# Block-product experts: the third product's copy taken ahead of the ReLU, the first two experts' weight work dealt anew, two maxima sent together

## The chip, the cores and the metric

The kernel runs on one core of one Trainium2 chip. The metric is the time of one execution on the device in microseconds (us), lower is better. Profiles are of single executions, taken by the hardware profiler. PE is the engine that multiplies matrices (TensorE), PEld its weight load, DVE the vector engine, ACT the scalar engine, POOL is GpSimd, SP the engine whose queue issues every DMA of this kernel. "n" below counts products of weights, "e" experts.

## What is computed

Attention, then a small dense layer, then eight experts that all see every token; the gate P is normalised by rows and columns eight times.

```python
def _moe2_ref(x, w_gate, w1, w2) -> np.ndarray:      # x (1152, 512), w1 (8, 512, 1024), w2 (8, 1024, 512)
    logits = x @ w_gate
    logits = logits - logits.max()
    P = np.exp(logits)
    for _ in range(8):
        P /= P.sum(1, keepdims=True) + 1e-09
        P /= P.sum(0, keepdims=True) + 1e-09
        P *= N / E
    out = np.zeros((N, D), dtype=np.float32)
    for e in range(E):
        h = np.maximum(x @ w1[e], 0.0)
        ye = h @ w2[e]
        out += P[:, e:e + 1] * ye
    return out.astype(np.float32)
```

The change lies in the experts alone.

## The kernel before

The kernel is one long program whose order is written out by hand: on each engine instructions run in the order in which the program issues them, and an instruction that waits holds all behind it. Every float32 matrix is split into a high and a low float16 part, and each product is the sum of three matmuls (high by high, high by low, low by high), scaled by powers of two that follow from the largest magnitude of each weight matrix.

**First matmul of an expert.** A column block n of w1 (four per expert, `up(n)`, n = 0 to 31) is a 2 by 2 block product with seven block products in place of eight (`prod`, L1229, 12 matmuls each), in the order x (A11 B11), z (A12 B21), y (S1 T1), x (S2 T2, added to the same bank), y (S4 B22, added to the same bank), x (S3 T3, added), z (A22 T4). Banks x, y and z hold the sums. ACT copies bank x as it stands after the first, fourth and sixth products and bank y after the third (`snap`, L1239: s1, s2, s3 and s5). DVE joins them (`join`, L1243, and the addition of L1291), ACT takes the ReLU's high half (`relu_hi`, L1247) and DVE its low half (`relu_lo`, L1252). A product that adds to a bank has to wait until the copy of that bank is done: the fifth product (y) waits for s5, the fourth and sixth (x) for s1 and s2. `then(0)` to `then(6)` mark seven segments of one `up`, in which other work is issued: tables `extra` (through `put`) and `between` name it.

**Second matmul.** The first expert's is done in two halves by `down_0` (nine token tiles of 128, `plain`, L1335, in two banks `d` of `ps_d`; ACT takes them out for h = 0, L1324, and DVE adds them for h = 1, L1326). The others use `down(e)`: again block products, four pairs of tiles i = 0 to 3, `more(i, k)` marks the places for other work, and each bank is added to `acc` by DVE (L1326) before the next product adds to it. The program order is up 0, up 1, up 2, `down_0(0)`, up 3, up 4, `down_0(1)`, up 5, up 6, up 7, `down(1)`, then four `up` and a `down` for each further expert.

**Weight work** beside all this: `prep(n, k)`, six steps for a w1 block (0: ACT scales, L919, and a load of block n + 4 is issued; 1, 2: DVE sums, L923 to L928; 3: ACT and POOL, L931 and L932; 4: ACT, L935; 5: POOL, L938), `p2(e, i)` for one of eight row blocks of w2 (two ACT steps, L1023 and L1024, one POOL step, L1025, and the load of the block after next), `split_b(e)` (eight DVE differences, L1316, called `t4`), `pe(e, i)`: the largest magnitude of one block (i < 4: w1, on DVE, L754; i from 4: w2, on ACT with a throw-away output `junk`, L102, that takes a bank `d` of `ps_d`). `send(e, kind)` reduces these (L788), writes 128 numbers to DRAM (`peaks`) and reads them back on all partitions (`all`); `power(e, kind)` takes the maximum of that on DVE (L751 and four small steps). Kind 1 is w1, kind 2 w2. The read is issued by SP only when the write has landed, and SP issues in order.

**What stood around expert 2's maxima.** Block maxima of w2 for e = 2 were taken in up 6 and up 7, sent in up 7, and taken and sent again in `down(1)`:

```python
                    if e == 1:                                   # in down(e), ahead of its first products
                        run(pe(2, 8, 9, 10, 11))
                        ...
                        if e == 1 and i == 0:                    # after two of the first tile pair's products
                            run(send(2, 2))
```

`power(2, 2)` followed at place (0, 4) of the same `down(1)`, and `pace` with `p2(2, 0..3)` behind it.

Of the kernel before, what the change touches and what calls it, by code (L numbers as in the profile page):

```python
# [23 lines left out]
DM = H * D  # L24
# [28 lines left out]
def make_body(stop=None):  # L53
    def body(tc, a):
# [21 lines left out]
        with ctx, tc.manual_schedule():  # L76
# [696 lines left out]
            def peak_e(e, i):  # L773

                if e < NE:
                    if e not in e_peak:
                        e_peak[e] = scl.tile([128, 12], F32, tag="pe", name="pe", bufs=3)
                    if i < 4:
                        peak(e_peak[e][:, i:i + 1], w1r[4 * e + i].rearrange("p b c f -> p (b c f)"))
                    else:  # L780
                        junk = jp[0].tile([128, DM], F32, tag="d", name="junk")
                        size(e_peak[e][:, i:i + 1], w2r[8 * e + i - 4], junk)

            def send_e(e, kind):
                if e < NE:
# [4 lines left out]
                    peak_get(("e", e, kind))  # L790

# [298 lines left out]
            with ExitStack() as ectx:  # L1090
# [92 lines left out]
                def m_spread():  # L1183
# [10 lines left out]
                           (1, 5): [p2(0)], (2, 0): [lambda: peak_all(*SC)], (2, 4): [p2(3)], (2, 5): [],  # L1194
                           (1, 6): [logits], (2, 1): [p2(1)], (2, 2): [flip], (2, 3): [p2(2), gate], (1, 2): [lambda: peak_get(SC[0])],
# [12 lines left out]
                def up(n, extra):  # L1208
# [150 lines left out]
                def down_0(h):  # L1359

                    parts = [(*h_t.pop(h), *w2t[0], 4 * h)]
                    kh = kh_t.pop(h)
                    if h == 0:
                        todo = {0: pe(1, 0, 1), 1: pe(1, 2, 3) + send(1, 1), 2: prep(3, 1) + pe(1, 4), 3: prep(3, 2, 3) + p2(0, 4),
                                4: prep(3, 4, 5) + p2(0, 5), 5: p2(0, 6) + pe(1, 5), 6: p2(0, 7) + pe(1, 6),
                                7: pe(1, 7), 8: power(1, 1) + prep(4, 0)}
                    else:
                        todo = {0: prep(5, 0), 1: prep(5, 1), 2: prep(5, 2, 3), 3: power(1, 2) + prep(5, 4, 5) + p2(1, 0),
                                4: p2(1, 1) + prep(6, 0), 5: prep(6, 1, 2) + p2(1, 2), 6: prep(6, 3, 4, 5) + p2(1, 3), 7: p2(1, 4, 5),
                                8: p2(1, 6, 7)}  # L1370
                    for t in range(NTT):
                        add(t, slice(0, DM), next(plain(t, parts)), kh, h, h == 0)
                        if h == 0 and t in (2, 4, 6) or h == 1 and t in (0, 2, 4, 6):
                            cols(banks[0])
                        if t in (0, 2, 4, 6):
                            rows()
                        run(todo.get(t, ()))

                def down(e):
# [59 lines left out]
                    if e == 1:  # L1439
                        run(pe(2, 8, 9, 10, 11))  # L1440
                    run(nxt[1] + nxt[2])
                    use_banks("ps_w")
                    for i in range(4):
# [17 lines left out]
                        if e == 1 and i == 0:  # L1461
                            run(send(2, 2))
# [30 lines left out]
                for n in range(4 * NE):  # L1493
# [6 lines left out]
                    if n == 2:  # L1500
                        put(1, prep(3, 0))
                    if n == 3:
                        for seg, k in ((0, 1), (1, 2), (2, 3), (3, 4), (3, 5)):
                            put(seg, prep(4, k))
                        for seg in range(4):
                            put(seg, pe(1, 8 + seg))
                        put(5, send(1, 2))
                    if n in (2, 4):
                        put(3, [lambda h=n // 2 - 1: gains(h)])
                    if n == 5:  # L1510
                        put(1, [lambda: cols(ps_d)])
                        put(0, prep(7, 0))
                        put(0, pe(2, 4))
# [3 lines left out]
                    if e:  # L1517
                        if q == 0 and e > 1:
                            put(0, pe(e + 1, 9))
                            put(2, t4(0, 1, 2))  # L1520
                            put(3, prep(n + 3, 0) + pe(e + 1, 10))
                            put(4, pe(e + 1, 11))
                            put(6, pe(e + 1, 0))
                        if q == 1:
                            put(0, prep(n + 2, 3) + (send(e + 1, 2) if e > 1 else []))
                            put(2, prep(n + 2, 1, 2) + (t4(3) if e > 1 else []))
                            put(6, pe(e + 1, 1))
                            if e == 1:
                                put(4, pe(2, 5))
                                put(5, t4(0))  # L1530
                                put(6, t4(1))
                        if q == 2:
                            put(2, prep(n + 1, 4, 5) + pe(e + 1, 2))
                            put(6, t4(2, 3) if e == 1 else t4(4, 5))
                            if e == 1:
                                for seg in (0, 1, 3, 4):
                                    put(seg, pe(2, (6, 7, 0, 8, 9)[seg]))
                                put(4, pe(2, 0))
                        if q == 3:
                            if e == 1:  # L1540
                                put(0, pe(2, 10, 11))
                                put(2, send(2, 2))
                            else:
                                put(0, power(e + 1, 2))
# [68 lines left out]
```

## Time and profile before

| what | us |
|---|---|
| median of 3 runs | 1071.03 (1070.78 to 1071.89) |
| the profiled execution | 1070.92 |
| its span, first to last instruction | 1069.1 |
| PE busy in the span | 1025.6 (96%) |
| DVE, ACT, POOL busy | 814.3, 613.1, 317.9 |
| mean granted clock of PE | 0.994 of full speed |

The stages of the experts in the span: up 0 begins at about 333, `down_0(0)` at 370, `down_0(1)` at 420, `down(1)` at 483, and from 548 on each expert takes 87. A row in brackets, as [0.83 <-ACT s L1239], says that the engine stood idle for 0.83 us before this instruction and that ACT's instruction of line 1239 ended that. Matmuls overlap; two short ones that follow each other without a wait start closer together than one lasts.

### The profile page before, as it was taken

To read this page: it belongs to the slowest core of one execution; us is meant where nothing else is said; L and a number is where in the kernel's file an instruction comes from. 1 tells how busy PE (TensorE), PEld (TensorE's weight loads), DVE (VectorE), ACT (ScalarE), POOL (GpSimd) and SP (SyncE) were. 2 spreads that over 40 slices of the span, in tenths; PEclk is the share of its full clock that TensorE was granted. 3 is DMA by queue.
4 is the path that set the end of the run, shared out by engine and by line. 5 is a ranking of instruction groups with operands and counts; after the bars stand their busy time and mean duration, and the time that the engine had idled before them with its cause. 6 is when DMAs were issued, how large, how long until landed. Compare 5 with 4: busy or idle time off the path is not lost.

```text
span 1069.1 us, 22013 instructions
## 1 busy us (share of the span) xinstructions
PE 1025.6 (96%) x8842; PEld 803.2 (75%) x8842; DVE 814.3 (76%) x1713; ACT 613.1 (57%) x1124; POOL 317.9 (30%) x228
## 2 busy tenths in 40 slices
PE   8999999999999989886899999999999999999998
PEld 3266777999998646464677887787787787788787
DVE  8977775999768767885858868867876886886774
ACT  9989885453347665752674475466456456545510
POOL 6952542232230132600340341151042034024100
PEclk9999999999999999999899999999999999999999
DMA  6986662434140211301320220111031022000001
GB/s 191 282 270 185 202 175 63 158 126 97 37 158 1 82 43 42 108 12 6 91 70 3 63 93 10 59 64 43 3 102 57 4 92 70 4 3 2 1 21 70
DMA packets 40179, 84.65 MB, mean 79 GB/s; under 512 B 8260, under 2 KB 11020, under 8 KB 40076
## 3 DMA queue, kind: packets, MB, share of 16 engines
q1 hardware_dynamic: 40076, 83.24, 25.4%
q8 instruction: 69, 1.13, 0.5%
q14 instruction: 34, 0.28, 0.1%
HBM read 69.92 MB, written 13.30 MB: 78 GB/s over the span
## 4 chain that ended last, share of the span: by engine, by line
PE 61%; DVE 11%; ACT 8%; issue 3%; DMA 2%; DVEq 0%; SPq 0%; ACTq 0%
PE m L602 11%; PE px L1408 6%; PE x L1229 6%; PE d L1335 6%; PE y L1229 5%; PE z L1229 4%; PE pz L1413 4%; PE pz L1408 4%; PE py L1408 4%; PE o L1067 4%; DVE s L1243 3%; DVE hl L1252 3%; ACT hh L1247 2%; PE px L1413 2%; PE py L1413 2%
## 5 line engine op out<-in xcount | busy, mean ns | idle before, releaser
L1229 PEld LDWEIGHTS <-w1h 128*128 128x128 f16 x1792 | 174.6, 98 | 66.9 <-issue 21.5
L1247 ACT ACTIVATE hh<-s 128x576 f16<-128x576 f32 x128 | 87.3, 682 | 131.9 <-DVE s L1243 104.9
L1252 DVE SCALAR_TENSOR_TENSOR hl<-s,hh 128x576 f16<-128x576 f32 x128 | 99.4, 779 | 43.1 <-ACT hh L1247 40.4
L938 POOL TENSOR_TENSOR w1l<-wf,w1h 128x1024 f16<-128x1024 f32 x32 | 68.3, 2134 | 185.1 <-ACT w1h L935 100.0
L1025 POOL TENSOR_TENSOR w2l<-w2r,w2h 128x512 f16<-128x512 f32 x60 | 70.2, 1180 | 170.8 <-ACT w2h L1024 168.8
L1408 PEld LDWEIGHTS <-s 128*128 128x128 f16 x896 | 88.3, 99 | 26.2 <-issue 14.9
L932 POOL TENSOR_TENSOR w1l<-wf,w1h 128x768 f16<-128x768 f32 x32 | 53.8, 1681 | 177.5 <-ACT w1h L931 121.0
L1229 PEld LDWEIGHTS <-w1l 128*128 128x128 f16 x896 | 87.6, 98 | 22.1
L1413 PEld LDWEIGHTS <-hh 128*128 128x128 f16 x896 | 87.7, 98 | 10.1
L1229 PE MATMUL x<-xth,w1h 128*128 128x288 f16 x384 | 78.4, 286 | 1.2 <-ACT s L1239 1.2
L1326 DVE SCALAR_TENSOR_TENSOR acc<-px,kh,acc 128x256 f32<-128x256 f32 x112 | 53.0, 479 | 33.6 <-PE px L1408 27.0
L1229 PE MATMUL x<-xth,w1l 128*128 128x288 f16 x384 | 78.4, 286 | 0.0
L1229 PE MATMUL x<-xtl,w1h 128*128 128x288 f16 x384 | 78.4, 286 | 0.0
L1239 ACT ACTIVATE s<-x,cx 128x576 f32<-128x576 f32 x96 | 70.1, 730 | 13.3 <-PE x L1229 12.9
L602 PE MATMUL m<-xh,wh 128*128 128x384 f32 x216 | 73.3, 340 | 0.0
L602 PE MATMUL m<-xl,wh 128*128 128x384 f32 x216 | 73.0, 338 | 0.0
L602 PE MATMUL m<-xh,wl 128*128 128x384 f32 x216 | 73.0, 338 | 0.0
L1408 PE MATMUL px<-t,s 128*128 128x256 f16 x448 | 58.9, 275 | 14.4 <-DVE acc L1326 14.3
L1243 DVE SCALAR_TENSOR_TENSOR s<-z,cx,s 128x576 f32<-128x576 f32 x64 | 52.2, 815 | 21.5 <-PE z L1229 15.0
L935 ACT ACTIVATE w1h<-wf 128x1024 f16<-128x1024 f32 x32 | 33.7, 1054 | 60.7 <-DVE wf L928 60.7
L1023 ACT ACTIVATE w2r<-w2r,pc 128x512 f32<-128x512 f32 x48 | 34.0, 708 | 59.4 <-DVE pc L1009 59.4
L494 DVE CUSTOM_DVE_ANT_0 ng<-sc,bias 128x576 f32<-128x576 f32 x72 | 51.6, 754 | 15.5 <-PE sc L481 7.4
(261 smaller groups left out, 2777.3 us busy)
## 6 DMA issues: line engine op xcount, KB each, us to landing
wr<-in_moe_w SPq DMA_DIRECT2D x50, 512.0 KB, 3.9
w2r<-in_moe_w SPq DMA_DIRECT2D x64, 256.0 KB, 2.9
bias_f<-bo SPq DMA_DIRECT2D x36, 295.5 KB, 4.5
bias<-bias_f SPq DMA_DIRECT2D x32, 288.0 KB, 3.6
qk<-in_qk SPq DMA_DIRECT2D x6, 576.0 KB, 4.9
wr<-in_moe_w_out SPq DMA_DIRECT2D x6, 512.0 KB, 3.3
v<-in_v SPq DMA_DIRECT2D x4, 640.0 KB, 4.9
bias<-bias_f SPq DMA_DIRECT2D x16, 144.0 KB, 5.1
```

The source lines that it names most:

```text
L602: T.matmul(out=p[:, :TG], lhsT=ws[:, 128 * c:128 * c + 128], rhs=xs[:, c, TG * g:TG * g + TG], start=(c == 0 and n == 0), stop=(c == 3 and ...
L932: G.tensor_tensor(out=lo[:, 0:3], in0=t[:, 1:4], in1=hi[:, 0:3], op=ALU.subtract)
L938: G.tensor_tensor(out=lo[:, 3:7], in0=t[:, 4:8], in1=hi[:, 3:7], op=ALU.subtract)
L1025: G.tensor_tensor(out=lo, in0=r, in1=hi, op=ALU.subtract)
L1229: T.matmul(out=ps[bank][:, s, :SH], lhsT=ws[:, i, c, :], rhs=xv[:, j, c, s * SH:s * SH + SH], start=(start and k == 0), stop=(k == 5), **kw)
L1239: A.activation(out=t, in_=src, func=AF.Identity, scale=c)
L1243: V.scalar_tensor_tensor(out=out, in0=z, scalar=scale, in1=out, op0=ALU.mult, op1=ALU.add)
L1247: A.activation(out=o, in_=src, func=AF.Relu)
L1252: V.scalar_tensor_tensor(out=l, in0=src, scalar=0.0, in1=o, op0=ALU.max, op1=ALU.subtract)
L1335: T.matmul(out=pd, lhsT=x, rhs=w, start=(y == 0), stop=(y == len(mm) - 1))
L1408: T.matmul(out=out, lhsT=x[z][:, j], rhs=w[z][:, j], start=(start and j == z == 0), stop=(j == 3 and z == 1), skip_group_check=True)
L1413: T.matmul(out=out, lhsT=(ha, hb)[j // 4][0][:, j % 4, 128 * t:128 * t + 128], rhs=wh[:, j, n], start=False, stop=(j == 7), skip_group_che ...
```

## The change

- In every `up` from n = 1 on, `relu_hi` of the first quarter is issued after the copy s5, as it was for n = 3 alone.
- `down(1)` loses the second set of maxima and the second `send(2, 2)`. A new `send_both(2)` in segment 1 of up 7 reduces both kinds, issues both writes, and then both reads. `power(2, 2)` moves from place (0, 4) to (0, 3).
- Where a block maximum of w2 is taken inside `down_0`, its throw-away output goes to a tile of the SBUF pool `sn` (tag s5) and no longer to a bank `d`.
- `prep`, `p2`, `pe`, `send` and `power` of experts 1 and 2 stand at other places of up 2 to up 7 and of `down_0`; the column normalisation that stood in up 5 stands at the last token tile of `down_0(0)`.
- For the experts from 2 on, the block maxima, the preparation steps and the differences of `split_b` are spread over other segments.

```diff
+                        if jp[-1] is sn:
+                            junk = sn.tile([128, 2, SH], F32, tag="s5", name="junk").rearrange("p s n -> p (s n)")[:, :DM]
+                        else:
+                            junk = jp[0].tile([128, DM], F32, tag="d", name="junk")
...
+            def send_both(e):
+                for k in (2, 1):
+                    m = scl.tile([128, 1], F32, tag="pj", name="pj", bufs=2)
+                    t = e_peak[e]
+                    V.tensor_reduce(out=m, in_=t[:, 0:4] if k == 1 else t[:, 4:12], op=ALU.max, axis=AX.X)
+                    peak_out(("e", e, k), m)
+                for k in (2, 1):
+                    peak_get(("e", e, k))
...
-                           (1, 6): [logits], (2, 1): [p2(1)], (2, 2): [flip], (2, 3): [p2(2), gate], (1, 2): [lambda: peak_get(SC[0])],
+                           (1, 6): [logits], (2, 2): [flip], (2, 3): [gate, p2(2)], (1, 2): [lambda: peak_get(SC[0])],
...
                         join(s1, z, c)
-                        if n != 3:
-                            relu_hi(0, 0, s1)
                         then(1)
                     s5 = snap("s5", prod(S1, T1, "y", True))
-                    if n == 3:
+                    if n > 0:
                         relu_hi(0, 0, s1)
-                    if n > 0:
                         relu_lo(0, 0, s1)
...
+                    jp.append(sn)
                     if h == 0:
-                        todo = {0: pe(1, 0, 1), 1: pe(1, 2, 3) + send(1, 1), 2: prep(3, 1) + pe(1, 4), 3: prep(3, 2, 3) + p2(0, 4),
+                        todo = {0: p2(0, 4) + pe(1, 0, 1), 1: p2(0, 5) + pe(1, 2, 3) + send(1, 1), 2: prep(3, 1) + p2(0, 6),
...
                     else:
-                        todo = {0: prep(5, 0), 1: prep(5, 1), 2: prep(5, 2, 3), 3: power(1, 2) + prep(5, 4, 5) + p2(1, 0),
+                        todo = {0: power(1, 2) + prep(5, 0, 3), 1: prep(5, 1, 2) + p2(1, 0), 2: prep(5, 4, 5) + p2(1, 1),
...
-                        at = (0, 3)
                         if e == 1:
-                            at = (0, 4)
-                            put(*at, power(2, 2))
-                        put(*at, [lambda: pace(e + 1)] + p2(e + 1, 0, 1, 2, 3))
+                            put(0, 3, power(2, 2))
+                        put(0, 3, [lambda: pace(e + 1)] + p2(e + 1, 0, 1, 2, 3))
...
-                    if e == 1:
-                        run(pe(2, 8, 9, 10, 11))
...
-                        if e == 1 and i == 0:
-                            run(send(2, 2))
...
-                    if n == 5:
-                        put(1, [lambda: cols(ps_d)])
...
+                    if n == 7:
+                        put(0, pe(2, 11) + t4(4))
+                        put(1, [lambda: send_both(2)] + t4(5, 6))
+                        put(2, t4(7))
```

How this stands on the engines, first on SP's queue between the last weight load ahead of expert 2's maxima and the loads behind them (peakse is a write of maxima, all the read back). Before:

```order
L60 DMA wr_6587<-in_moe_w 128x1024
L60 DMA peakse_6879<-pj 128x1
L60 DMA all<-peakse_6879 128x128
L60 DMA peakse_6885<-pj 128x1
L60 DMA all<-peakse_6885 128x128
L60 DMA peakse_7031<-pj 128x1
L60 DMA all<-peakse_7031 128x128
L60 DMA w2r<-in_moe_w 128x512 x4
```

And in the changed kernel, the same place of SP's queue:

```order
L60 DMA wr_6651<-in_moe_w 128x1024
L60 DMA peakse_6863<-pj 128x1
L60 DMA peakse_6867<-pj 128x1
L60 DMA all<-peakse_6863 128x128
L60 DMA all<-peakse_6867 128x128
L60 DMA w2r<-in_moe_w 128x512 x4
```

Three pairs of write and read, each read ahead of the next write, became two writes followed by two reads.

DVE in `down(1)`, from the last sums of the first tile pair (L1401) to the second `power`. Before:

```order
L1326 SCALAR_TENSOR_TENSOR acc<-px,kh,acc 128x256
L1401 TENSOR_TENSOR s<-hh 128x512
L1401 TENSOR_TENSOR s<-hl 128x512
L1326 SCALAR_TENSOR_TENSOR acc<-pz,kh,acc 128x256 x2
L1326 SCALAR_TENSOR_TENSOR acc<-py,kh,acc 128x256
L751 TENSOR_REDUCE pm<-all 128x1
L727 TENSOR_SCALAR pm<-pm 128x1
L728 TENSOR_SCALAR pw<-pm 128x1
L730 TENSOR_SCALAR pw<-pm 128x1
L824 TENSOR_SCALAR pw<-pw 128x1
L1009 COPY pc<-pw 128x1
L1326 SCALAR_TENSOR_TENSOR acc<-px,kh,acc 128x256 x2
```

The same place in the changed kernel (line numbers are those of the changed file; L1412 is the sums, L1335 the additions to acc):

```order
L1335 SCALAR_TENSOR_TENSOR acc<-px,kh,acc 128x256
L1412 TENSOR_TENSOR s<-hh 128x512
L1412 TENSOR_TENSOR s<-hl 128x512
L751 TENSOR_REDUCE pm<-all 128x1
L727 TENSOR_SCALAR pm<-pm 128x1
L728 TENSOR_SCALAR pw<-pm 128x1
L730 TENSOR_SCALAR pw<-pm 128x1
L836 TENSOR_SCALAR pw<-pw 128x1
L1021 COPY pc<-pw 128x1
L1335 SCALAR_TENSOR_TENSOR acc<-pz,kh,acc 128x256 x2
L1335 SCALAR_TENSOR_TENSOR acc<-py,kh,acc 128x256
L1335 SCALAR_TENSOR_TENSOR acc<-px,kh,acc 128x256 x2
```

The maximum's five steps and the copy `pace` moved ahead of three additions.

ACT in up 11, the last `up` of expert 2, in which s_7950 is s1, s_7988 is s5, s_8015 is s2 and s_8043 is s3. Before:

```order
L1239 ACTIVATE s_7950<-x,cx 128x576
L1247 ACTIVATE hh<-s_7950 128x576
L1239 ACTIVATE s_7988<-y,cx 128x576
L1239 ACTIVATE s_8015<-x,cx 128x576
L1247 ACTIVATE hh<-s_8015 128x576
L1239 ACTIVATE s_8043<-x,cx 128x576
```

The same in the changed kernel (L1251 is the copy, L1259 the ReLU; s_7936 is s1, s_7973 s5, s_7996 s2, s_8029 s3):

```order
L1251 ACTIVATE s_7936<-x,cx 128x576
L1251 ACTIVATE s_7973<-y,cx 128x576
L1259 ACTIVATE hh<-s_7936 128x576
L1251 ACTIVATE s_7996<-x,cx 128x576
L1259 ACTIVATE hh<-s_7996 128x576
L1251 ACTIVATE s_8029<-x,cx 128x576
```

The copy of bank y now stands ahead of the ReLU of s1, and s2's copy behind that ReLU.

## Rows read from the trace of the kernel before

**Rows 1.** Waits of PE, 343 to 485 us: total us, times, longest.

```profile
PE y L1229 <- ACT s L1239: 4.0, 4, 1.4
PE d L1335 <- ACT acc L1324: 2.8, 4, 0.8
PE z L1229 <- DVE s L1243: 1.3, 2, 0.8
PE x L1229 <- ACT s L1239: 1.2, 2, 0.8
PE d L1335 <- DVE acc L1326: 1.2, 1, 1.2
...
PE pc L1164 <- DVE acc L1326: 0.6, 1, 0.6
```

**Rows 2.** Waits of PE, 485 to 548 us, the same columns.

```profile
PE px L1408 <- DVE acc L1326: 14.3, 2, 14.1
```

**Rows 3.** Waits of PE, 548 to 983 us, the same columns.

```profile
PE y L1229 <- ACT s L1239: 5.4, 10, 1.0
```

**Rows 4.** Timeline of PE in `down(1)`: start, duration, instruction, idle before it.

```profile
512.76 1.86 PE L1408 MATMUL px<-t,s 128*128 128x256 f16 x8 [14.05 <-DVE acc L1326]
```

**Rows 5.** Timeline of DVE in `down(1)`, around its longest wait.

```profile
495.26 0.48 DVE L1326 SCALAR_TENSOR_TENSOR acc<-py,kh,acc 128x256 f32<-128x256 f32 x1
...
510.89 0.29 DVE L751 TENSOR_REDUCE pm<-all 128x1 f32<-128x128 f32 x1 [15.15 <-DMA all<-peakse]
```

**Rows 6.** Timeline of SP's queue: issues of expert 2's maxima, first and last pair.

```profile
478.75 0.33 SPq L60 DMA_DIRECT2D peakse<-pj  x1
486.46 0.33 SPq L60 DMA_DIRECT2D all<-peakse  x1
...
497.10 0.32 SPq L60 DMA_DIRECT2D peakse<-pj  x1
506.57 0.32 SPq L60 DMA_DIRECT2D all<-peakse  x1
```

**Rows 7.** Two stretches: length, busy time by engine, PE's clock, DMA.

```profile
498.70:512.80 14.10, 0.05 (x2) 0.03 (x1) 1.80 (x9) 0.80 (x2) 0.00 (x0) 0.68 0.25 9
512.80:520.00 7.20, 7.20 (x46) 5.48 (x46) 6.34 (x14) 6.54 (x10) 4.69 (x4) 0.67 0.46 114
```

**Rows 8.** Timeline of three engines in up 11, around its fifth product.

```profile
581.15 0.82 DVE L1243 SCALAR_TENSOR_TENSOR s<-z,cx,s 128x576 f32<-128x576 f32 x1
...
581.88 0.41 PE L1229 MATMUL x<-xtl,w1h 128*128 128x288 f16 x2
...
582.00 0.68 ACT L1247 ACTIVATE hh<-s 128x576 f16<-128x576 f32 x1 [2.91 <-DVE s L1243]
582.12 0.41 PE L1229 MATMUL x<-xth,w1l 128*128 128x288 f16 x2
582.59 0.72 ACT L1239 ACTIVATE s<-y,cx 128x576 f32<-128x576 f32 x1
...
583.37 0.40 PE L1229 MATMUL y<-xth,w1h 128*128 128x288 f16 x2 [0.83 <-ACT s L1239]
```

**Rows 9.** Timeline of PE in up 10, at its fifth product.

```profile
571.43 0.41 PE L1229 MATMUL x<-xth,w1l 128*128 128x288 f16 x2
571.97 0.41 PE L1229 MATMUL y<-xth,w1h 128*128 128x288 f16 x2
```

**Rows 10.** Timeline of ACT and PE in `down_0(0)`, third and fourth token tile.

```profile
379.20 0.59 ACT L102 ACTIVATE junk<-w2r 128x512 f32<-128x512 f32 x1
379.35 0.38 PE L1335 MATMUL d<-w2h,hh 128*128 128x512 f16 x1 [0.60 <-ACT acc L1324]
```

**Rows 11.** Timeline of POOL and DVE in `down(1)`, second tile pair.

```profile
513.42 5.02 POOL L1025 TENSOR_TENSOR w2l<-w2r,w2h 128x512 f16<-128x512 f32 x4 [43.15 <-ACT w2h L1024]
...
517.35 1.38 DVE L1401 TENSOR_TENSOR s<-s,hh 128x512 f16<-128x512 f16 x1
518.65 0.41 DVE L1401 TENSOR_TENSOR s<-s,hl 128x512 f16<-128x512 f16 x1
```

More of the change, by code (lines that the diff above doesn't have):

```diff
@@ L1500, in body @@
                     if n == 2:
-                        put(1, prep(3, 0))
+                        put(3, prep(3, 0))
                     if n == 3:
[L1503 to L1507, printed above, removed]
+                        put(0, prep(4, 3) + pe(1, 11))
+                        put(1, prep(4, 1))
+                        put(2, send(1, 2) + prep(4, 2))
+                        put(3, prep(4, 4, 5))
+                    if n == 4:
+                        put(1, pe(2, 0))
                     if n in (2, 4):
                         put(3, [lambda h=n // 2 - 1: gains(h)])
-                    if n == 5:
-                        put(1, [lambda: cols(ps_d)])
-                        put(0, prep(7, 0))
-                        put(0, pe(2, 4))
                     if e and q == (1 if e == 1 else 0):
@@ new lines, in body @@
+                    if n == 5:
+                        put(0, prep(6, 4, 5) + pe(2, 7))
+                        put(1, pe(2, 2))
+                        put(2, t4(0))
+                        put(3, prep(7, 0))
+                        put(4, prep(7, 1))
+                        put(5, pe(2, 8))
+                        put(6, prep(7, 2))
+                    if n == 6:
+                        put(0, prep(7, 3, 4, 5))
+                        put(1, pe(2, 3))
+                        put(2, t4(1))
+                        put(3, pe(2, 9))
+                        put(4, t4(2))
+                        put(5, pe(2, 10))
+                        put(6, t4(3))
@@ new lines, in body @@
+                    if n == 7:
+                        put(0, pe(2, 11) + t4(4))
+                        put(1, [lambda: send_both(2)] + t4(5, 6))
+                        put(2, t4(7))
+                    if e > 1:
+                        if q == 0:
+                            put(0, pe(e + 1, 9, 10))
+                            put(1, pe(e + 1, 0))
+                            put(2, t4(0))
+                            put(3, prep(n + 3, 0))
+                            put(4, t4(1))
+                            put(6, t4(2))
+                        if q == 1:
+                            put(0, prep(n + 2, 3) + pe(e + 1, 11))
+                            put(1, send(e + 1, 2) + pe(e + 1, 1))
+                            put(2, prep(n + 2, 1))
+                            put(4, prep(n + 2, 2))
+                            put(6, t4(3))
+                        if q == 2:
+                            put(0, prep(n + 1, 4, 5))
+                            put(1, pe(e + 1, 2))
+                            put(2, t4(4))
+                            put(4, t4(5))
+                        if q == 3:
+                            put(0, power(e + 1, 2))
@@ L1545, in body @@
                             put(1, pe(e + 1, 3))
[L1546 removed]
+                            put(2, send(e + 1, 1) + t4(6))
+                            put(4, t4(7))
+                    if e and q == 3:
+                        put(4, [lambda: gains(e + 1)])
                     up(n, extra)
```

42 lines of the change are left out of this document (8 added, 34 removed).

## The prediction, made before the changed kernel was run

> **What bounds the kernel now.** I read first where PE stands idle, because it is busy for 96% of the span: only what PE waits for can be won, and a faster DVE or ACT is worth nothing where PE doesn't wait. From 343 us on, where the change begins, there are three kinds of wait.
>
> One is a single hole. PE waits once for 14.05 us in `down(1)` [rows 4], which is nearly the whole of its waits between 485 and 548 us [rows 2]. It waits for an addition to `acc`, and DVE has that addition in its queue behind `power(2, 2)`, which sits idle for 15.15 us until the maxima are read back [rows 5]. SP's queue tells why they come so late: the first write is issued at 478.75, its read at 486.46, and the last pair, the repeated one, at 497.10 and 506.57 [rows 6]. One round is 7.7 to 9.5 us for the write and 4.3 until DVE can go on (506.57 to 510.89); three went one after the other. The hole costs more than its length: after it the granted clock is 0.67 over 7.2 us [rows 7], so part of the matmuls ran at the lower of the two levels, 1.2 in place of 2.4 GHz. That is 7.2 x 0.33 = 2.4 us.
>
> The second is regular: from 548 to 983 us PE waits ten times, two per expert for five experts, always for ACT's copy of bank y, 5.4 us in all [rows 3]. Up 11 shows one [rows 8]: the third product had ended before, but ACT did `relu_hi` first, which waited 2.91 us for DVE's join (581.15, 0.82), and only then the copy (582.59, 0.72). PE's next product on y started at 583.37.
>
> The third is the first two experts, 343 to 485 us: fifteen waits of up to 1.4 us, of which one view has those that I count [rows 1].
>
> What a wait costs is a little more than its bracket. In up 11 the pairs of matmuls start 0.24 us apart (581.88, 582.12); the next would have come at 582.37 and came at 583.37, so the loss is 1.00 where the bracket says 0.83. I add 0.17 to each wait.
>
> **The hole.** The second set of maxima and its write and read go. What is left is two writes one behind the other, then two reads, issued one segment earlier in up 7 than the first write was. I don't count on that and take 478.75 as the write's time. The read is then issued at 486.5 to 488.2 and its data is there 4.3 later, at 490.8 to 492.5; the second read is some 0.4 behind. DVE comes to `power(2, 2)` shortly before its addition of 495.26 [rows 5], a little earlier now as it stands ahead of three additions of 0.48. So 2 to 4 us are in hand. The addition for which PE waits is needed at 512.76 - 14.05 = 498.7, so a landing up to about 495.5 costs nothing. The six DVE steps moved ahead are hidden in the same way. The hole goes whole: 14.05 + 0.17 + 2.4 for the clock = **16.6 us**. Behind it `p2(2, 0..3)` follows on ACT and POOL as it does in the later experts, where PE had no wait in `down` (its ten waits there are all of y) [rows 3].
>
> **The copy ahead of the ReLU.** In up 11 the copy could have begun at 581.1, when its product was done, and been over by 581.8, ahead of 582.37. So the y waits go: 5.4 + 10 x 0.17 = 7.1 us. There is a shorter one without a bracket in up 10, where 571.97 - 571.43 = 0.54 in place of 0.24 [rows 9]: 0.3 for each of five experts, 1.5. What becomes late instead is `relu_hi`, by one copy, and behind it the copy s2, which the sixth product needs one product later (12 matmuls, six pairs of 0.245, are 1.47 us). In up 11 that ReLU would start at 582.00 as before, and s2 at about 582.7, done at 583.4; the sixth product starts at 583.84. So it holds, with 0.4 us to spare in the worst up; in the others DVE's join comes earlier. DVE's `relu_lo` gets up to 1.5 us later, and the spreading of `split_b` and `prep` takes work from between it and the next join. **8.6 us**. Both ends: nothing, if the wait only moves on, and 10 if the x and z products, which follow from the same copies, lose their short delays too. I take 1.5 of these, as much as the short one at y: **10.1 us**.
>
> **The first two experts.** The four y waits [rows 1] are of the same kind: 4.0 + 0.7 = 4.7. The four at d are made by `junk`: it takes one of two banks d, and the next token tile has to wait for the ACT addition of the tile just done (the row at 379.35 is one, beside the junk at 379.20 [rows 10]); with junk in SBUF they go, 2.8 + 0.7 = 3.5. The normalisation's pc that waited for DVE in up 5 moves to a place where DVE's additions don't lie ahead of it: 0.6 + 0.2 = 0.8. Of the x and z waits (1.2 + 0.3 and 1.3 + 0.3) I take half, 1.5, since the causes, ACT's junk ahead of a copy and POOL's work beside DVE, are moved and not gone. The wait of d for DVE, 1.2, stays: its tiles in `down_0(1)` get the same eight row blocks, spread thinner, but also a 1.2 us maximum. The change adds a cost: `power(1, 1)` moves up one token tile, and the write of these maxima now stands on SP behind two loads that wait for POOL (`p2(0, 4)` and `p2(0, 5)`). Behind `power` queue the column sums on DVE, and `prep(4, 0)`, one junk and the last addition on ACT, and the first copy of up 3. From below it is zero, if the write goes out as before; from above 1.8, the spread of the write (9.5 against 7.7). I take 0.5. Sum 4.7 + 3.5 + 0.8 + 1.5 - 0.5 = **10.0 us**. The ends are 5 (only half of each) and 13 (all).
>
> **Sum.** 16.6 + 10.1 + 10.0 = 36.7. The profiled execution took 1070.92, 0.1 under the median of the runs, so it stands for them: 1070.9 - 36.7 = **1034.2, say 1034**.
>
> **Rivals.** *The second maximum is late.* If the second write queues for a whole write time behind the first, its read is issued at 478.75 + 2 x 9.5 = 497.7 and lands at 502. `power(2, 1)` then holds DVE ahead of an addition that PE needs three products of 0.87 later, at about 501: 2 us, **1036**. For it: three rounds here took more each when another transfer was just ahead (9.5 against 7.7). Against: a write of 0.5 KB is nearly all latency.
>
> *The wait only moves on.* If s2 or the joins are late by what s5 was, terms of 10.1 don't come: **1044**. For it: the ReLU still waits for the same join. Against: 1.47 us more until the need.
>
> *POOL's work in front of DVE.* In `down_0(1)` eight POOL steps of `p2` now start two tiles earlier, beside the normalisation and the additions. A DVE sum takes 1.38 beside such a step and 0.41 after it [rows 11]: 0.97 more. Hit once per step, on the path, this is 8 x 0.97 = 7.8: **1042**. Against: each addition may be one token tile late, and POOL's work is thinner at the end, where the wait of 1.2 was. The Trainium skill (SBUF — State Buffer, Who interferes with whom) has a rule that speaks against this move: a DVE instruction with two SBUF inputs and a POOL instruction that reads SBUF lock each other out, whole instructions long, so each meeting would cost up to the 1.26 of one POOL step (5.02 / 4), and eight 10 us, 1044. The trace agrees in kind, with 0.97.
>
> *The change doesn't do what it says.* If the reads still go round after round so that the last lands where it did, the hole stays: 1034 + 16.6 = **1051**. Against: the order on SP.
>
> *Slower.* One mechanism: DVE gets so late by the ReLU's shift that every up from n = 4 on makes PE wait at its next x. It decides from 36.7 / 28 = 1.3 us per up; with a whole product, 1.47, the time is 1034 + 41 = **1075**. Against: DVE is busy for 76% of the span, and PE's waits on it in the ups are few.
>
> **How the numbers follow.** Forecast (1027 to 1039) 0.66, late second maximum 0.10, wait moves on 0.09, POOL 0.07, hole stays 0.04, slower 0.02, and 0.02 for below 1027, where every wait from 343 us on would be gone. The range has the forecast, the late maximum, POOL and most of the moved wait: 1027 to 1043. What a measurement of this kernel can tell from no change is about 0.2%, 2 us; all cases but one are faster by more: 0.97, and 0.01 and 0.02 for the rest.
>
> **What would show it.** After: no wait of PE over 2 us behind 343, the clock at 1.00 through `down(1)`; two writes of maxima within 1 us in up 7, and `power(2, 2)` without idle time ahead of it; no wait of y for ACT in the later experts, which take 85 us each in place of 87; no wait of d for ACT in `down_0(0)`. Wrong it is if x or z products wait in place of y, if `power` waits for a read, or if DVE's additions in `down_0(1)` hold PE for more than 3 us.

## The result, and the profile after

The changed kernel takes 1035.67 us (median of 4 runs, 1034.88 to 1036.39) where the kernel before took 1071.46 beside it (1070.78 to 1072.50): ratio 0.9665, 95% interval 0.9648 to 0.9682. Forecast was 1034, with 1027 to 1043. The profiled execution took 1036.12, 34.8 less than that of before (1070.92).

The profile page after, from its first part (busy time, share of the span, instructions):

```profile
PE 1017.4 (98%) x8842; PEld 802.7 (78%) x8842; DVE 813.1 (79%) x1712; ACT 612.5 (59%) x1116; POOL 319.0 (31%) x228
```

PE is busy for 98% of a shorter span.

All waits of PE from 340 us to the end (total us, times, longest):

```profile
PE pc L1176 <- DVE P L1172: 3.3, 2, 2.3
PE y L1241 <- ACT s L1251: 1.5, 5, 0.4
PE z L1241 <- DVE s L1255: 1.3, 1, 1.3
PE pm L1161 <- DVE nm L1157: 0.4, 1, 0.4
PE d L1344 <- DVE acc L1335: 0.2, 1, 0.2
```

Against [rows 1 to 3]: the hole in `down(1)` is gone, and so are every wait of d for ACT and all y waits of the first two experts; of the ten y waits of the later experts five are left, 1.5 us in place of 5.4. New is pc, the column sums of the normalisation, with 3.3 us.

**The hole.** SP's queue around expert 2's maxima, then DVE at the two `power` steps of `down(1)`:

```profile
470.18 0.80 SPq L60 DMA_DIRECT2D peakse<-pj  x2
...
478.08 0.84 SPq L60 DMA_DIRECT2D all<-peakse  x2
```

```profile
485.49 0.28 DVE L751 TENSOR_REDUCE pm<-all 128x1 f32<-128x128 f32 x1
...
489.26 0.28 DVE L751 TENSOR_REDUCE pm<-all 128x1 f32<-128x128 f32 x1
```

Three rounds on SP [rows 6] have become one: both writes issued within 0.80 us, both reads 7.9 us later. Neither maximum has a bracket, where the one in [rows 5] had 15.15.

**The later experts.** PE's one wait in expert 2, in up 8, and ACT's queue ahead of it:

```profile
525.71 0.41 PE L1241 MATMUL y<-xth,w1h 128*128 128x288 f16 x2 [0.28 <-ACT s L1251]
```

```profile
524.30 0.60 ACT L102 ACTIVATE junk<-w2r 128x512 f32<-128x512 f32 x1 [1.90 <-DMA w2r<-in_moe_w]
...
524.93 0.72 ACT L1251 ACTIVATE s<-y,cx 128x576 f32<-128x576 f32 x1
```

What is left of the y waits is another thing than in [rows 8]: the copy stands behind a junk that waits for its load. The last of the five such rows, and two of the kernel before, the y waits of up 9 and of up 13:

```profile
866.62 0.40 PE L1241 MATMUL y<-xth,w1h 128*128 128x288 f16 x2 [0.34 <-ACT s L1251]
```

```profile
561.20 0.40 PE L1229 MATMUL y<-xth,w1h 128*128 128x288 f16 x2 [0.20 <-ACT s L1239]
...
648.32 0.41 PE L1229 MATMUL y<-xth,w1h 128*128 128x288 f16 x2 [0.20 <-ACT s L1239]
```

An expert takes (866.62 - 525.71) / 4 = 85.23 us now and took 648.32 - 561.20 = 87.12 before. Over five experts that is 9.5 us.

**The new wait.** PE, DVE and POOL in `down_0(1)`:

```profile
431.51 0.47 PE L1176 MATMUL pc<-P,ones 128*128 128x72 f32 x2 [2.30 <-DVE P L1172]
```

```profile
427.03 2.11 DVE L1180 SCALAR_TENSOR_TENSOR P<-P,col 128x72 f32<-128x72 f32 x1
429.17 0.23 DVE L1169 TENSOR_REDUCE row<-P 128x9 f32<-128x72 f32 x1
429.44 0.75 DVE L1170 TENSOR_SCALAR row<-row 128x9 f32<-128x9 f32 x1
...
430.48 0.89 DVE L1172 TENSOR_TENSOR P<-P,row 128x72 f32<-128x72 f32 x1
431.29 0.74 DVE L1335 SCALAR_TENSOR_TENSOR acc<-d,kh,acc 128x512 f32<-128x512 f32 x1
```

```profile
426.91 2.13 POOL L950 TENSOR_TENSOR w1l<-wf,w1h 128x1024 f16<-128x1024 f32 x1 [1.45 <-ACT w1h L947]
429.00 3.39 POOL L1037 TENSOR_TENSOR w2l<-w2r,w2h 128x512 f16<-128x512 f32 x3
```

Read the ends: L1180, a step on 72 numbers a partition, begins at 427.03 and ends at 429.14; POOL's step ends at 429.04. L1170 ends at 430.19 and L1172 at 431.37, where the first and the second of POOL's three steps end (430.13 and 431.26, if the three take 3.39 / 3 = 1.13 each). Each DVE step ends when POOL's does. The Trainium skill (SBUF — State Buffer, Who interferes with whom) says that a DVE instruction with two SBUF inputs, or a `tensor_scalar` in a two-port mode, and a POOL instruction that reads SBUF hold each other off for a whole instruction, and that a DVE reduction doesn't take part. The trace agrees: L1180 and L1172, with two inputs in SBUF, and L1170, a `tensor_scalar`, end with POOL's steps, and L1169, a reduction, took 0.23 beside POOL. So does the addition L1335, one of whose inputs comes from PSUM: 0.74 beside POOL, as elsewhere. The kernel before has such a meeting too, at a place where PE didn't wait for it, beside POOL's step of 443.23 (2.14):

```profile
443.34 2.12 DVE L1168 SCALAR_TENSOR_TENSOR P<-P,col 128x72 f32<-128x72 f32 x1
```

The clock behind that wait (windows: stretch, length, busy time by engine, granted clock, DMA):

```profile
431.00:432.00 1.00, 0.47 (x2) 0.33 (x3) 1.00 (x3) 0.97 (x2) 1.00 (x2) 0.86 0.69 137
432.00:433.00 1.00, 0.92 (x3) 0.36 (x3) 1.00 (x2) 1.00 (x2) 0.69 (x2) 0.50 0.43 154
433.00:434.00 1.00, 1.00 (x4) 0.33 (x3) 0.97 (x4) 0.97 (x3) 1.00 (x1) 0.50 1.05 342
434.00:435.00 1.00, 1.00 (x3) 0.29 (x2) 0.93 (x3) 0.97 (x2) 1.00 (x2) 0.50 0.88 297
435.00:436.00 1.00, 1.00 (x6) 0.49 (x5) 0.93 (x3) 1.00 (x4) 1.00 (x2) 0.93 0.87 315
```

After 2.3 us of idle PE the clock stood at the lower level (1.2 GHz) for 3 us and a little: 0.14 + 3 x 0.50 + 0.07 = 1.7 us of lost work. It doesn't happen in every execution: two of the four have a mean clock of 1.000 (1034.88 and 1035.22 us), two of 0.997 and 0.998 (1036.12 and 1036.39). These pairs lie 1.2 us apart, so that is about what it adds to the time, less than the lost work.

**By stretch.** The times at which PE starts `up 0`, `down(1)` and `up 8`, and at which its last product ends, in the two traces:

| stretch | before | after | less by |
|---|---|---|---|
| start to up 0 | 333.40 | 332.55 | 0.85 |
| up 0 to `down(1)` (482.66, 475.51) | 149.26 | 142.96 | 6.30 |
| `down(1)` to up 8 (544.26, 519.38) | 61.60 | 43.87 | 17.73 |
| up 8 to the end of the last product (1065.35, 1030.44) | 521.09 | 511.06 | 10.03 |

The 0.85 us ahead of up 0 are not of the change, which begins later. In `e1_one_send`, which has the code of before there, up 0 starts at 332.14.

### The profile page after: what moved, and what is told of

The parts are those of the page before. It is cut to its first block, busy times and chain, and to the rows that moved or that the text cites. A ratio compares the mean times of both kernels' runs of the same rounds, so it can differ in the third digit from the quotient of the medians.

```text
span 1034.3 us, 22001 instructions
## 1 busy us (share of the span) xinstructions
PE 1017.4 (98%) x8842; PEld 802.7 (78%) x8842; DVE 813.1 (79%) x1712; ACT 612.5 (59%) x1116; POOL 319.0 (31%) x228
## 3 DMA queue, kind: packets, MB, share of 16 engines
q8 instruction: 69, 1.13, 0.5%
## 4 chain that ended last, share of the span: by engine, by line
PE 44%; POOL 3%; issue 2%; DMA 1%; ACT 1%; DVE 0%; ACTq 0%
PE x L1241 9%; PE y L1241 6%; PE z L1241 6%; PE px L1419 6%; PE pz L1419 4%; PE py L1419 4%; PE pz L1424 3%; PE d L1344 2%; PE px L1424 2%; PE py L1424 2%; DMA w2r<-in_moe_w 1%; POOL w2l L1037 1%; POOL w1l L950 1%; POOL w1l L944 1%; ACT junk L102 0%
## 5 line engine op out<-in xcount | busy, mean ns | idle before, releaser
L1259 ACT ACTIVATE hh<-s 128x576 f16<-128x576 f32 x128 | 87.0, 680 | 77.6 <-DVE s L1255 48.9
L1424 PEld LDWEIGHTS <-hh 128*128 128x128 f16 x896 | 87.7, 98 | 10.1
L1251 ACT ACTIVATE s<-x,cx 128x576 f32<-128x576 f32 x96 | 70.5, 734 | 18.1 <-PE x L1241 17.6
L1335 DVE SCALAR_TENSOR_TENSOR acc<-px,kh,acc 128x256 f32<-128x256 f32 x112 | 53.1, 479 | 34.1 <-PE px L1419 27.8
```

The costliest lines, as they stand in the source:

```text
L1251: A.activation(out=t, in_=src, func=AF.Identity, scale=c)
L1259: A.activation(out=o, in_=src, func=AF.Relu)
L1335: V.scalar_tensor_tensor(out=o, in0=ps, scalar=s, in1=o, op0=ALU.mult, op1=ALU.add)
L1424: T.matmul(out=out, lhsT=(ha, hb)[j // 4][0][:, j % 4, 128 * t:128 * t + 128], rhs=wh[:, j, n], start=False, stop=(j == 7), skip_group_che ...
```

## The experiments

The theory: the prediction's three terms (the repeated maxima, ACT's order, the new deal) each bring what they were sized at. Times in us are compared with the changed kernel's, which took 1035.67 on one chip and 1035.44 on another; the kernel before took 1071.46 on the first and 1067.5 to 1068.2 on those of the experiments. Part of this difference seems to be the hole itself: 14.05 us in [rows 4], 12.38 in the trace of `e4_before_new_relu`, which leaves the hole's code alone but has another order on ACT ahead of it. So a gain over the kernel before is 3 to 4 us smaller in what follows.

| run | what | us | ratio to before, 95% |
|---|---|---|---|
| e1_one_send | before without the second maxima | 1054.60 | 0.9875 (0.9858 to 0.9891) |
| e2_both | that, with `send_both` | 1054.24 | 0.9871 (0.9856 to 0.9885) |
| e3_after_old_relu | after with the old order on ACT | 1039.77 | 0.9734 (0.9719 to 0.9748) |
| e4_before_new_relu | before with the new order on ACT | 1071.76 | 1.0035 (1.0022 to 1.0048) |
| after_again | after | 1035.44 | 0.9696 (0.9682 to 0.9711) |
| e5_junk_bank | after with junk in a bank d | 1040.29 | 0.9746 (0.9729 to 0.9762) |
| e6_no_pool_p2 | after without POOL in `p2(1, i)` | 1032.35 | 0.9669 (0.9655 to 0.9684) |
| v1_round_moved | after, a normalisation round moved | 1034.25 | 0.9685 (0.9670 to 0.9699) |
| v2_pool_later | that, two POOL steps later | 1031.82 | 0.9662 (0.9646 to 0.9679) |
| v3_rows_later | that, row steps a tile later | 1030.97 | 0.9659 (0.9645 to 0.9674) |

### The repeated maxima

```diff
-                    if e == 1:
-                        run(pe(2, 8, 9, 10, 11))
...
-                        if e == 1 and i == 0:
-                            run(send(2, 2))
```

> The kernel before, without the second taking of expert 2's w2 maxima and without the second send in down(1); all else as before. Theory (the hole of 14.05 us is the third round of write and read, and its clock): the hole goes, 1071.5 - 16.6 = 1055, plus about 1 us, since the w1 maxima still go in a round of their own and are back at about 500.7, so that power(2, 1) holds DVE's additions for a product that PE starts at 501.3: 1056. Rival (the hole comes of something else late in the same stretch, such as ACT's accumulator rows or the weights): under 5 us gained, over 1066.

Measured 1054.60. SP's queue, and PE's waits from 485 to 560 us:

```profile
477.48 0.33 SPq L60 DMA_DIRECT2D peakse<-pj  x1
...
484.94 0.33 SPq L60 DMA_DIRECT2D all<-peakse  x1
485.39 0.35 SPq L60 DMA_DIRECT2D peakse<-pj  x1
...
494.21 0.32 SPq L60 DMA_DIRECT2D all<-peakse  x1
```

```profile
PE px L1408 <- DVE acc L1326: 0.7, 2, 0.4
PE py L1408 <- DVE acc L1326: 0.6, 1, 0.6
```

The theory holds: two rounds are early enough, the third made the hole. The gain against the kernel before on this chip is 1068.03 - 1054.60 = 13.4; by the prediction's rule it should be the bracket of `e4_before_new_relu` on the same chip, 12.38, + 0.17 + 2.4 for the clock, less the 1.3 us of small waits that are left: 13.65.

In `e2_both` `send_both` replaced the two sends, in segment 2 of up 7:

```diff
-                                put(2, send(2, 2))
+                                put(2, [lambda: send_both(2)])
```

> As e1_one_send, with the two writes one behind the other and then the two reads, as the change has it (in segment 2 of up 7, where the writes stood before). Theory (the writes overlap, each 7.7 to 9.5 us from its own issue): both reads back by 492.5, no idle time of DVE ahead of either power, 1055, that is 1 us under e1_one_send. Rival (the second write queues for a whole write behind the first): the second read is back at about 502, as late as in e1_one_send, and the two take the same time.

Measured 1054.24. PE's wait at py is gone, and the two px waits are 0.9 in place of 0.7. The difference of 0.36 us is less than the runs can tell. So of this part it is the second taking that costs; how the two writes are sent is worth at most that.

### ACT's order and the new deal

```diff
                         join(s1, z, c)
+                        if n != 3:
+                            relu_hi(0, 0, s1)
                         then(1)
                     s5 = snap("s5", prod(S1, T1, "y", True))
+                    if n == 3:
+                        relu_hi(0, 0, s1)
                     if n > 0:
-                        relu_hi(0, 0, s1)
                         relu_lo(0, 0, s1)
```

> The changed kernel with the ReLU's order of before (ahead of the copy of bank y, except in up 3). Theory (the order gave the late experts' gain): the waits of y for ACT return, two per expert from 2 on and in the first ups, 1035.7 + 10 = 1046. Rival (the gain came from spreading DVE's differences and maxima over the segments, so that the join ahead of the ReLU is early anyway): 1036 to 1038.

Measured 1039.77, which is 4.1 to 4.3 above the changed kernel, between the two expectations. From 520 us on PE waits five times at y, 4.2 us in all; the first row:

```profile
526.20 0.41 PE L1241 MATMUL y<-xth,w1h 128*128 128x288 f16 x2 [0.85 <-ACT s L1251]
```

The fifth and last stands at 869.29: an expert takes (869.29 - 526.20) / 4 = 85.77. Without the new order the deal still brings 87.12 - 85.77 = 1.35 of the 1.89 us per expert. In the first two experts two y waits return, 1.0 us in all, where the kernel before had 4.0.

The reverse, the kernel before with only the new order (the same lines changed the other way):

> The kernel before with the ReLU behind the copy of bank y in every up from 1 on; all else, the hole too, as before. Theory (the order alone): 7.1 us of bracketed y waits in the late experts, 1.5 without brackets and 4.7 in the first ups go, 1071.5 - 13 = 1058. Rival (without the new spread DVE is late, so that the wait moves on to the copy s2 and the next x): 1066 or more, with waits of x for ACT in place of y.

Measured 1071.76, 3.7 slower than the kernel before: the rival. PE's waits from 548 to 984 us; then PE at the start of up 9, and DVE and ACT in up 8 ahead of it:

```profile
PE x L1229 <- ACT s L1239: 6.3, 10, 0.8
```

```profile
550.62 0.41 PE L1229 MATMUL x<-xth,w1h 128*128 128x288 f16 x2 [0.80 <-ACT s L1239]
```

```profile
545.32 0.76 DVE L1252 SCALAR_TENSOR_TENSOR hl<-s,hh 128x576 f16<-128x576 f32 x1 [1.57 <-ACT hh L1247]
545.99 0.69 DVE L1313 TENSOR_TENSOR tb<-w2l 128x1024 f16<-128x1024 f16 x1
...
547.80 0.81 DVE L1243 SCALAR_TENSOR_TENSOR s<-y,cx,s 128x576 f32<-128x576 f32 x1
```

```profile
548.64 0.68 ACT L1247 ACTIVATE hh<-s 128x576 f16<-128x576 f32 x1 [0.81 <-DVE s L1243]
...
549.84 0.72 ACT L1239 ACTIVATE s<-x,cx 128x576 f32<-128x576 f32 x1
```

And the `relu_lo` of up 8 in the kernel before:

```profile
549.39 0.76 DVE L1252 SCALAR_TENSOR_TENSOR hl<-s,hh 128x576 f16<-128x576 f32 x1 [0.75 <-ACT hh L1247]
```

Ten waits of y became ten waits of x, 6.3 us for 5.4. The chain of the longer five: the ReLU of s1, one copy later, holds DVE's `relu_lo` for 1.57 us, where the trace of before has 0.75 at this place. Behind it stand three of `split_b`'s differences (0.68 each) and then the join of y, so the join is late, behind it ACT's ReLU of s2, a junk, and the copy s3, for which the first product of the next up waits. The rows repeat at 638.48 and 726.36, 87.87 us an expert, 0.75 more than before. The new deal leaves one of the three between the two steps (526.93 in the changed kernel, with the join at 527.53). So the order alone loses 3.7 and the order on top of the new deal gains 4.1 to 4.3. The loss comes wholly from the later experts: in the first two the y waits fall from 4.0 to 0.8 us, and `down(1)` comes 2.6 us sooner after up 0 than in `e1_one_send`, which has the order of before; from up 8 to the last product it takes 526.59 in place of 521.09.

### junk's bank

```diff
-                    jp.append(sn)
...
-                    jp.pop()
```

> The changed kernel with junk put back into a bank d in down_0 (seven of them in down_0(0), three in down_0(1)). Theory (the bank makes PE wait for ACT's or DVE's addition of the tile just done): waits of d for ACT of 0.5 to 0.8 us come back behind most of the junks of down_0(0), 2.5 to 4 us in all, and the time is 2 to 5 us above the changed kernel's (1035.5): 1038 to 1040. Rival (ACT, which now takes the junks elsewhere in the stretch, is early enough, so the bank costs nothing): within 1 us, no wait of d for ACT over 0.3.

Measured 1040.29, 4.6 to 4.9 above the changed kernel (which wasn't timed beside it). PE's waits from 340 us on, those of d for ACT, and the larger one beside ACT's queue:

```profile
PE d L1344 <- ACT junk L102: 3.4, 2, 2.2
...
PE d L1344 <- ACT acc L1333: 1.4, 2, 0.8
```

```profile
386.75 0.38 PE L1344 MATMUL d<-w2h,hh 128*128 128x512 f16 x1 [2.23 <-ACT junk L102]
```

```profile
385.99 0.59 ACT L102 ACTIVATE junk<-w2r 128x512 f32<-128x512 f32 x1
...
386.60 0.58 ACT L102 ACTIVATE junk<-w2r 128x512 f32<-128x512 f32 x1
```

The bank theory holds, with a time a little above its 1038 to 1040 and with a second mechanism: where two junks follow each other, PE waits for the junk itself and not only for the addition. There are four such waits, 4.8 us in all, fewer and longer than expected.

### POOL beside the normalisation

In `e6_no_pool_p2` ACT writes zeros where POOL wrote the low half of expert 1's w2, so that half is missing from its result.

```diff
+                            if 8 <= i < 16:
+                                A.activation(out=lo, in_=r, func=AF.Identity, scale=0.0)
+                            else:
-                            G.tensor_tensor(out=lo, in0=r, in1=hi, op=ALU.subtract)
+                                G.tensor_tensor(out=lo, in0=r, in1=hi, op=ALU.subtract)
```

> The changed kernel with POOL taken out of expert 1's w2 preparation: the low halves of its eight row blocks are written by ACT as zeros (scale 0) in place of POOL's difference, so the low half of w2 of expert 1 is left out of the result. Theory (POOL's steps stand in the way of DVE's normalisation chain in down_0(1)): the wait of pc there, 2.3 us in the changed kernel, falls under 1 us, the clock dip behind it goes, and the time is 1.5 to 3.5 us below the changed kernel's, 1032 to 1034. Rival (the chain of the normalisation round is too long by itself, or DVE's additions stand ahead of it): the wait stays at 1.5 us or more and the time within 1 us. The wait of z in up 3 (1.29) and of pc in down_0(0) (1.02) stay in both, since POOL's work there is prep of w1 and isn't touched.

> The changed kernel once more, to stand beside the next three on one chip. Theory: 1035 to 1036.5, with one wait of pc for DVE of about 2.3 us in down_0(1) and the granted clock falling to its lower level for some 3 us right behind it, unless the clock happens not to fall, which would take about 1.2 us off.

`after_again` took 1035.44, as expected: in its profiled execution the wait of pc is 2.29 us and the clock is low from 432 to 436; two of its four runs have a mean clock of 1.000.

`e6_no_pool_p2` took 1032.35, 3.1 less. PE's wait in `down_0(1)`, and the same DVE steps:

```profile
429.05 0.41 PE L1179 MATMUL pc<-P,ones 128*128 128x72 f32 x2 [0.59 <-DVE P L1175]
```

```profile
425.81 2.10 DVE L1183 SCALAR_TENSOR_TENSOR P<-P,col 128x72 f32<-128x72 f32 x1
...
428.22 0.17 DVE L1173 TENSOR_SCALAR row<-row 128x9 f32<-128x9 f32 x1
...
428.67 0.23 DVE L1175 TENSOR_TENSOR P<-P,row 128x72 f32<-128x72 f32 x1
```

The two steps that stood beside `p2` fall from 0.75 to 0.17 and from 0.89 to 0.23; the first, beside POOL's step of `prep` (425.70 to 427.83, left as it was), still takes 2.10. PE waits 0.59 in place of 2.30, and the clock stays at 1.00 there. The waits of z behind up 3 (1.29) and of pc in `down_0(0)` (1.02) stay, as expected. Beside the two runs of `after_again` with a mean clock of 1.000 (1034.71 and 1034.85) the gain is 2.4, of which the bracket is 1.7; the rest of the 3.1 is the clock of the other two.

### Moving the round, POOL's steps and the row steps

```diff
-                        if h == 0 and t in (2, 4, 6, 8) or h == 1 and t in (0, 2, 4, 6):
+                        if h == 0 and t in (2, 4, 6, 8) or h == 1 and t in (0, 4, 7):
                             cols(banks[0])
-                        if t in (0, 2, 4) or h == 0 and t in (6, 8):
+                        if t in (0, 4) or h == 0 and t in (2, 6, 8):
                             rows()
...
                     if n == 4:
-                        put(1, pe(2, 0))
+                        put(1, [lambda: cols(ps_d), rows])
+                        put(2, pe(2, 0))
```

> The changed kernel with one of four normalisation rounds moved from down_0(1) to segment 1 of up 4, the remaining column sums of down_0(1) standing at token tiles 0, 4 and 7 and its row steps at 0 and 4. Theory (three rounds within six tiles, beside POOL's steps, are what PE waits for): the 2.3 us wait and the clock dip go, up 4 gets no wait over 0.5 us in return, time 2.5 to 4 us below the changed kernel's, 1031.5 to 1033.5. Rival (the wait goes with the round to up 4, or to the round at tile 4): within 1 us of the changed kernel's.

Measured 1034.25, 1.2 less, under what was expected. PE's waits from 340 us on, the largest group:

```profile
PE d L1344 <- DVE acc L1335: 2.5, 3, 1.7
```

The pc wait of `down_0(1)` and the clock dip are gone (of pc only the 1.0 in `down_0(0)` is left), but DVE is as late as it was: now an addition that stands behind the row steps holds a bank d. Beside the two runs of `after_again` without a clock dip the gain is only 0.5, so most of the 1.2 is the clock. The wait moved, as the rival says, though not to where it says. The second version adds:

```diff
-                        put(3, prep(4, 4, 5))
+                        put(5, prep(4, 4, 5))
...
-                                3: prep(3, 2, 3) + p2(0, 7), 4: prep(3, 4, 5) + pe(1, 4), 5: pe(1, 5, 6), 6: pe(1, 7, 8),
+                                3: prep(3, 2, 3) + p2(0, 7), 4: pe(1, 4), 5: prep(3, 4, 5) + pe(1, 5, 6), 6: pe(1, 7, 8),
```

> As the version before, and POOL's last step of the w1 blocks 3 and 4 put later: in down_0(0) from token tile 4 to 5, in up 3 from segment 3 to 5. Theory (these two POOL steps lock DVE's 385.70 and 402.58 for 1.8 and 2.2 us): the waits of pc in down_0(0) (1.02) and of z in up 3 (1.29) go, 2 to 2.6 us further, 1029 to 1031.5. Rival (POOL's step then locks the next DVE step in the same way, or the wait is for DVE's queue): the two waits stay at over 0.5 us or come up elsewhere, and the gain is under 1 us.

Measured 1031.82, 2.4 less again, as the theory has it. PE's waits from 340 us on, but for one of 0.4 at pm:

```profile
PE d L1344 <- DVE acc L1335: 2.8, 3, 1.7
PE y L1241 <- ACT s L1251: 1.7, 5, 0.4
```

The z wait that up 3's work makes (1.3, in the second product of up 4) and the pc wait of `down_0(0)` (1.0) have gone with POOL's two steps; the step of `down_0(0)` that took 1.79 in the changed kernel (L1172 at 385.70) takes 0.23 here (at 385.40). The third version adds:

```diff
-                        if t in (0, 4) or h == 0 and t in (2, 6, 8):
+                        if (t in (0, 2, 4, 6, 8) if h == 0 else t in (1, 5)):
```

> As the second version (round moved, POOL later), and in down_0(1) the row steps one token tile behind the column sums, at tiles 1 and 5 in place of 0 and 4, so that DVE's additions of tiles 1 and 5 stand ahead of them. Theory (the waits of d for DVE there, 0.9 and 1.7 us, come from additions queued behind row steps which POOL's steps lengthen, 1.60 in place of 0.17 us for one): both fall under 0.5 us, 1.5 to 2.5 us less than that version's 1031.8, 1029.3 to 1030.3. Rival (the locked DVE steps are late in any order and PE then waits for them at the next column sums): within 0.6 us of 1031.8, with waits of pc in place of d.

Measured 1030.97, on another chip than the version before: 0.85 less, and the intervals of the two ratios overlap, so whether it is faster than `v2_pool_later` stays open. The trace says why the expected 1.5 to 2.5 didn't come: of the waits of d for DVE (2.8 us) two are left, 1.20 and 0.58, one of them from `prep`'s sums that now stand ahead of the addition and take 1.38 in place of 0.41 beside a `p2` step. Both versions beat the changed kernel, by 3.6 and 4.5 us (against 1035.44, which for `v3_rows_later` is a figure from another chip).

## Why the prediction was right, and where not

**The hole: right, 16.6 us.** Nothing of it is left in the trace, and `e1_one_send` agrees with the rule for its price (bracket + 0.17 + clock) within 0.3 us, if the bracket on that chip is the 12.38 of `e4_before_new_relu`. `down(1)` became 17.7 shorter; where the other 1.1 come from isn't shown. The step that 2 to 4 us were in hand holds too: neither maximum has idle time ahead of it. The rival "the second maximum is late" fell: two writes issued together land together, and even one after the other they cost PE only 1.3 us.

**The later experts: size right, cause half wrong.** 10.1 was forecast; 9.5 came by the five experts' rows, at 85.2 us an expert, and 10.0 from up 8 to the end. The step that failed is "so it holds, with 0.4 us to spare in the worst up; in the others DVE's join comes earlier". In the deal of before it doesn't hold: `e4_before_new_relu` shows the rival "the wait only moves on" there, with ten x waits. That the size was met all the same is luck. The prediction named the new spread in half a sentence and gave it no term; by `e3_after_old_relu` it carries 1.35 x 5 = 6.8 of the 9.5, and the order the other 2.7, which it can bring only on top of it. Which part of the new deal carries the 6.8 isn't shown. The check went from the ReLU to s2, in up 11 alone, and there it holds: `e4_before_new_relu` has no wait in up 11. In up 8 the way goes on through `relu_lo`, `split_b` and the next join to s3. Also, one y wait per expert is left, of 0.2 to 0.4, behind a junk that the new deal put there.

**The first two experts: 10.0 forecast, 6.3 came** (up 0 to `down(1)`, in an execution with the clock dip). The waits at y (4.7) and of junk (3.5) are gone whole; putting junk back costs 4.6 to 4.9 in the new order. At y the order is not the only cause here either: alone it leaves 0.8 us of the 4.0, and the new deal without it leaves 1.0. The wait of d for DVE, which was to stay at 1.2, went to 0.2. `power(1, 1)`, with 0.5, showed no wait. Of z and x waits 1.3 is left of 2.5, as forecast: one at z, in the second product of up 4, where it was 0.80 before and is 1.29 now, behind a DVE step of up 3 that one POOL step holds up. What was mis-sized is the normalisation: the term of +0.8 for pc turned into waits of 3.3, and about 1.2 more for the clock in half of the executions. That was the rival "POOL's work in front of DVE", named with the right place and mechanism at 7.8, and worth 3.1 by `e6_no_pool_p2`: not every meeting is on the path, but those that are last a whole POOL step, up to 2.11 - 0.23 = 1.88 more in place of the 0.97 taken, and the longest is beside a step of `prep`, not of `p2`. The argument against it, "POOL's work is thinner", failed. In `down_0(1)` DVE takes the tiles out, so nothing ties ACT's steps of `p2` to the token tiles. ACT first stood still for 3.65 us until `power(1, 2)` was done:

```profile
422.82 0.72 ACT L1035 ACTIVATE w2r<-w2r,pw 128x512 f32<-128x512 f32 x1 [3.65 <-DVE pw L836]
```

It stood 1.57 more for a sum of `prep`, and from 425.78 to 439.5 it worked without a pause. So POOL's steps of the second, third and fourth row block came one behind the other, from 429.00 to 432.39, beside a round of the normalisation.

**The sum.** 36.7 was forecast, 34.8 came in the profiled executions, and that they lie so close is in part luck: the first two experts fell short by 3.7, `down(1)` brought 1.1 more than its term, and 0.85 lie ahead of the change.

**The signs named ahead.** Clock 1.00 through `down(1)`, two writes within 1 us, no idle time at `power(2, 2)`, no wait of d for ACT, 85 us an expert: all as said. "No wait of PE over 2 us behind 343" failed by one, the 2.30 at 431.51. "No y wait in the later experts" failed by five short ones.

## What to carry to other kernels

An order of two instructions on one engine is worth what the queue behind it allows: cost a swap with everything that stands between it and the next need in every repeat, not in one, and ask whether another edit of the same change makes the room for it. Spreading work over places in program order spreads it in time only on an engine that something paces; one that was held once and then waits for nothing does it all in one bunch, as ACT did here from 425.78 on. Short steps on a chain that PE waits for should not stand beside long POOL steps that read SBUF: moving two POOL steps by one and two places was worth 2.4 us here.

## What the hardware showed that I had not expected

A DVE step on 72 numbers a partition took 2.11 us in place of 0.23 when it began 0.12 us behind a POOL step of 2.13; in `e6_no_pool_p2`, which leaves that POOL step in place, it took 2.10. Even one on 9 numbers (L1170) took 0.75, and 0.17 once the POOL step beside it was gone.

A wait of 2.30 us in `down_0(1)` was followed by 3 us at the lower clock in the profile above. The same wait at the same place in `e3_after_old_relu` was not; its row, and the windows line of the stretch behind it, with a granted clock of 1.00:

```profile
432.11 0.41 PE L1176 MATMUL pc<-P,ones 128*128 128x72 f32 x2 [2.29 <-DVE P L1172]
```

```profile
433.00:435.00 2.00, 2.00 (x11) 0.88 (x9) 1.95 (x4) 1.97 (x4) 1.69 (x2) 1.00 0.64 206
```

Nor was one of 2.23 in `e5_junk_bank`, at 386.75 (1.00 in every stretch up to 397). The length of a wait alone didn't decide; what did isn't shown.

The same kernel before took 1071.5 on one chip and 1067.5 to 1068.2 on three others, while the changed kernel took 1035.7 on the first and 1035.4 on one of the others. The kernel before has no trace on the other chips, but `e1_one_send`, on one of them, has its code up to `down(1)` and again from up 8: there up 0 starts 1.26 us earlier, and up 8 to the last product takes 0.36 less. With the 1.7 by which the hole of `e4_before_new_relu` is shorter, that is 3.3 of the 3.4 us (1071.46 - 1068.03). What makes these stretches shorter there stays open.
